# Products of keys and values on the two column halves of TensorE: linear attention and a gated feed-forward in one kernel

## The chip, the cores and the metric

The kernel runs on one core of a Trainium2 chip. The core has a matrix engine (TensorE, PE in the profile; its weight loads are listed as PEld), a vector engine (VectorE, DVE), an activation engine (ScalarE, ACT), GpSimd (POOL) and SyncE (SP). TensorE reads its operands from SBUF and writes to PSUM, from which VectorE and ScalarE copy results back. Each engine works through its own list of instructions in order and waits on the others by semaphores; transfers from and to the chip's memory are issued on queues of SP and POOL. The metric is the device time of one execution in microseconds (us), lower is better.

## The reference, cut to what matters

```python
# q, k, v: (8 batches, 8 heads, 576 positions, 64)
phi = lambda x: np.where(x > 0, x, np.exp(x) - 1.0) + 1.0
q_p, k_p = phi(q), phi(k)
kv  = np.einsum('bhsd,bhse->bhde', k_p, v)      # per head: 64x64
z   = np.sum(k_p, axis=2)                       # per head: 64
num = np.einsum('bhsd,bhde->bhse', q_p, kv)
den = np.einsum('bhsd,bhd->bhs', q_p, z)[..., None] + 1e-06
x   = (num / den).transpose(0, 2, 1, 3).reshape(8 * 576, 512)
a, b = x @ w1, x @ w2                           # 512 -> 1024
out = (a * b @ w3) @ w_out                      # 1024 -> 1024 -> 512
```

Since nothing stands between the last two products, the kernel forms w3 @ w_out once and applies it as one matrix of 1024x512.

## The kernel before, in words

**Tiling.** Each batch has 576 positions: 512 of them make four tiles of 128 (index j, 0 to 3), and the 64 that remain are put together two batches at a time (names that end in r; kr and vrz hold keys and values of the remainder, and vrz is zero outside its own batch's rows). Heads go in pairs: hp is 0 to 3, with u = 0, 1 for the two heads of a pair. phi is max(x, 0) + 1 on VectorE (step t), exp on ScalarE (step x), and the minimum of the two on VectorE (step m, one for each pair, 128x512). Values are copied to bf16 into one buffer, vt, which has a column of ones behind each head's 64 columns, so that a product with keys gives kv and z together: 65 columns for a head (E1), 130 for a pair (PW).

**The product kv.** Step kv takes one batch and one pair. Its weights are the keys of both heads of the pair (128 positions x 128 columns), its moving operand the values of both heads (130 columns), and it makes five matmuls that accumulate in PSUM: four for j (L238) and one for the remainder (L241). The result is 128x130, of which the diagonal blocks, head 0's keys with head 0's values and head 1's with head 1's, are wanted; the two others are computed and not read. Steps kc (two or four pairs) and kh (one pair) copy the wanted blocks to the tile kvb, one copy for each half r of the rows, on ScalarE (a) or VectorE (v). kvb is zero outside its diagonal blocks.

**What follows.** Step na multiplies the queries of a pair with its kvb (four matmuls of 130 columns, L291), nd divides by the denominator on VectorE (L297 to L299) into xn, and xp with xc, or a transposing DMA (xd), turns the result into xt. Step f is a feed-forward step: for one block of 128 columns it makes four matmuls of 512 columns with w1 (a_ps) and four with w2 (b_ps) (L400). ac copies a_ps to SBUF on ScalarE (L414), ab multiplies it with b_ps on VectorE (L419). Step o makes eight matmuls of 512 columns (L425), one for each ab block in the order 0 to 7; oc copies its result out and st stores it. PSUM is used as four banks in turn for f, o and the transposes (mm_ps) and two double banks in turn for kv and na (at_ps).

**The order of the work.** It is written out by hand. The string ORDER is read from left to right; each word, such as `kv:2,1` (batch 2, pair 1) or `ab:1,5` (batch 1, block 5), appends the instructions of its step to the lists of the engines it uses. The tool that builds the kernel adds semaphore waits where one step needs another's data or buffer, and leaves the order as it is. So a step placed later stands later in its engine's list. Attention of batch b + 1 and later stands among the feed-forward steps of batch b and before. The kv products of batches 2 to 7 stand, one or two at a time, among f, o and xp steps. `v:3,0,4,v` copies heads 0 to 3 of batch 3's values into vt on VectorE; as vt is a single buffer, it follows the products of batch 2 that read these heads. GATES adds a few waits between loads and is not concerned.

Of the kernel before, what the change touches and what calls it, by code (L numbers as in the profile page):

```python
# [18 lines left out]
def kernel(  # L19
# [376 lines left out]
    def f_part(c, f, cs):  # L396
        for n, w in (("a", w1_sb), ("b", w2_sb)):
            o = got(ps, (n, c, f), mm_ps, [P, NCH], F32, "mm", n + "_ps")
            for kc in cs:
                nc.tensor.matmul(o, w[:, kc, f * P:(f + 1) * P], xt_of(c)[:, :, kc, :],  # L400
                                 start=(kc == 0), stop=(kc == KC - 1))
# [80 lines left out]
    st:0,3,g x:k,2,0,4 kv:2,2 ab:1,7 f:1,0 m:k,2,0,1 m:k,2,0,0 ac:1,0,a t:q,2,0,4 x:q,2,0,4 kv:2,0 f:1,4
    ab:1,0 x:q,2,4,4 ld:q,3,0,8,s t:q,2,4,4 m:q,2,0,0 ac:1,4,a m:q,2,0,1 f:1,6 m:q,2,4,2 m:q,2,4,3
    ab:1,4 ac:1,6,a qd:2 f:1,2 ab:1,6 ac:1,2,a kv:2,1 ab:1,2 f:1,1 v:3,0,4,v ac:1,1,a f:1,3 x:q,3,4,4
    t:q,3,0,4 lp:v,2,s ab:1,1 ac:1,3,a tr:k,2,2 xr:k,2,2 t:q,3,4,4 f:1,5 ld:k,3,0,8,s x:q,3,0,4 ab:1,3
# [5 lines left out]
    kc:3,0,2,0,v st:1,2,g x:q,4,4,4 kc:3,0,2,1,v f:2,0 vr:5,v t:q,4,4,4 ac:2,0,a f:2,1 ab:2,0 ac:2,1,a
    m:q,4,4,2 m:q,4,0,0 na:3,0 m:q,4,0,1 na:3,2 f:2,6 ab:2,1 nd:3,2 ac:2,6,a nd:3,0 f:2,4 v:4,4,4,a
    v:4,0,4,v ab:2,6 ac:2,4,a na:3,3 m:q,4,4,3 ld:k,4,0,8,s na:3,1 ab:2,4 f:2,7 lp:k,3,s nd:3,3 ac:2,7,a
    nd:3,1 qd:4 f:2,3 ab:2,7 ac:2,3,a f:2,2 ab:2,3 ac:2,2,a t:k,4,0,4 x:k,4,4,4 f:2,5 t:k,4,4,4
    x:k,4,0,4 ab:2,2 ld:k,5,0,8,s xd:3 m:k,4,4,2 ac:2,5,a m:k,4,4,3 kv:4,2 m:k,4,0,0 kv:4,3 ab:2,5 o:2,2
    m:k,4,0,1 xr:k,3,2 tr:k,3,2 kv:4,1 mr:k,3,2 oc:2,2,a kv:4,0 o:2,3 kc:4,0,2,0,a st:2,2,g kc:4,0,2,1,a
    na:4,0 oc:2,3,a na:4,3 o:2,1 nd:4,0 x:k,5,0,4 st:2,3,g nd:4,3 ld:q,5,0,8,s x:k,5,4,4 t:k,5,4,4
    na:4,1 na:4,2 oc:2,1,a o:2,0 nd:4,1 st:2,1,g m:k,5,4,2 nd:4,2 ld:v,5,0,8,s oc:2,0,a t:k,5,0,4 xd:4
    st:2,0,g m:k,5,0,1 m:k,5,4,3 m:k,5,0,0 f:3,7 ac:3,7,a f:3,2 ab:3,7 ac:3,2,a x:q,5,4,4 t:q,5,0,4
    f:3,4 ab:3,2 x:q,5,0,4 t:q,5,4,4 f:3,3 m:q,5,4,2 ac:3,4,a m:q,5,0,1 ab:3,4 ac:3,3,a lp:v,3,s  # L500
    m:q,5,4,3 v:5,4,4,a m:q,5,0,0 f:3,0 ab:3,3 v:5,0,4,a qd:5 ac:3,0,a kv:5,3 kv:5,0 ab:3,0 kv:5,1
    kv:5,2 f:3,6 kc:5,0,2,0,a kc:5,0,2,1,v ac:3,6,a ld:v,6,0,8,s f:4,6 ab:3,6 ac:4,6,a f:4,7 ab:4,6
    vr:6,a vr:7,v ac:4,7,a f:4,3 ab:4,7 ac:4,3,a na:5,2 na:5,0 ab:4,3 f:4,0 nd:5,2 v:6,0,4,a v:6,4,4,v
    ac:4,0,a lp:q,0,s na:5,3 nd:5,0 f:4,4 ab:4,0 ld:q,6,0,8,s ac:4,4,a nd:5,3 ld:k,6,0,8,s f:4,1 ab:4,4
    ac:4,1,a f:4,2 ld:v,7,0,8,s ab:4,1 ac:4,2,a f:4,5 ab:4,2 x:q,6,4,4 t:q,6,4,4 t:q,6,0,4 x:q,6,0,4
    f:3,1 m:q,6,4,2 m:q,6,4,3 ac:4,5,a m:q,6,0,0 m:q,6,0,1 ac:3,1,a ab:4,5 o:4,0 qd:6 x:k,6,4,4 ab:3,1
    t:k,6,0,4 x:k,6,0,4 o:4,3 t:k,6,4,4 oc:4,0,a tr:q,0,2 xr:q,0,2 m:k,6,4,2 st:4,0,g m:k,6,4,3
    ld:k,7,0,8,s m:k,6,0,1 kv:6,2 oc:4,3,v o:4,2 mr:q,0,2 st:4,3,g m:k,6,0,0 kv:6,0 oc:4,2,v kv:6,1
    qdr:0 kv:6,3 v:7,0,4,a o:4,1 st:4,2,g kc:6,0,2,1,v v:7,4,4,v kc:6,0,2,0,v na:5,1 oc:4,1,v f:3,5
    nd:5,1 st:4,1,g ac:3,5,a xd:5 na:6,0 na:6,3 ab:3,5 o:3,1 nd:6,3 nd:6,0 o:3,3 oc:3,1,v x:k,7,0,4  # L510
    t:k,7,4,4 st:3,1,g ld:q,7,0,8,s x:k,7,4,4 t:k,7,0,4 o:3,0 m:k,7,0,1 oc:3,3,a m:k,7,0,0 m:k,7,4,2
    st:3,3,g m:k,7,4,3 kv:7,0 oc:3,0,a kv:7,2 kv:7,3 st:3,0,g kv:7,1 o:3,2 kc:7,0,2,1,v kc:7,0,2,0,v
    na:6,2 oc:3,2,v na:6,1 f:5,7 nd:6,1 st:3,2,g nd:6,2 ac:5,7,a f:5,6 xd:6 ab:5,7 ac:5,6,a nar:0 nar:1
    ab:5,6 f:5,3 x:q,7,4,4 t:q,7,4,4 lp:q,1,s x:q,7,0,4 ndr:1 f:5,2 m:q,7,4,3 ac:5,3,a m:q,7,4,2 ab:5,3
    ac:5,2,a t:q,7,0,4 f:5,4 m:q,7,0,0 ab:5,2 ac:5,4,a m:q,7,0,1 ndr:0 qd:7 f:6,1 ab:5,4 ac:6,1,a f:6,7
    xdr:0 ab:6,1 ac:6,7,a lp:q,2,s f:6,4 ab:6,7 lp:q,3,s ac:6,4,a f:6,2 ab:6,4 ac:6,2,a na:7,3 na:7,2
    ab:6,2 f:6,6 nd:7,2 xr:q,1,2 tr:q,1,2 ac:6,6,a mr:q,1,2 f:6,5 nd:7,3 qdr:1 ab:6,6 ac:6,5,a na:7,0
    f:5,1 ab:6,5 nd:7,0 ac:5,1,a f:6,0 ab:5,1 ac:6,0,a f:5,0 ab:6,0 xr:q,2,2 tr:q,2,2 ac:5,0,a mr:q,2,2
    na:7,1 qdr:2 f:5,5 ab:5,0 xr:q,3,2 tr:q,3,2 nd:7,1 ac:5,5,a nar:2 mr:q,3,2 xd:7 nar:3 ab:5,5 o:5,1
    ndr:2 ndr:3 o:5,0 qdr:3 oc:5,1,a st:5,1,g xdr:1 o:5,2 oc:5,0,a st:5,0,g o:5,3 oc:5,2,a st:5,2,g  # L520
    f:7,0 oc:5,3,a st:5,3,g ac:7,0,a nar:4 f:7,6 ab:7,0 ndr:4 ac:7,6,a nar:5 f:7,3 ab:7,6 ndr:5 ac:7,3,a
    xdr:2 nar:7 f:7,1 ab:7,3 ac:7,1,a ndr:7 f:7,4 ab:7,1 ac:7,4,a f:7,7 ab:7,4 ac:7,7,a nar:6 f:7,5
    ab:7,7 ndr:6 ac:7,5,a xdr:3 f:7,2 ab:7,5 ac:7,2,a f:6,3 ab:7,2 ac:6,3,a o:7,1 ab:6,3 o:7,2 oc:7,1,a
    st:7,1,s o:6,1 oc:7,2,a st:7,2,s f:8,5 oc:6,1,a st:6,1,s ac:8,5,a f:8,0 ab:8,5 ac:8,0,a f:8,3 ab:8,0
    ac:8,3,a f:8,6 ab:8,3 ac:8,6,a f:8,7 ab:8,6 ac:8,7,a f:8,1 ab:8,7 ac:8,1,a ab:8,1 o:6,0 o:6,3
# [44 lines left out]
```

## Time and profile before

| | |
|---|---|
| median of 5 runs | 252.67 us (252.09 to 252.85) |
| the profiled execution | 252.16 us, span from first to last instruction 250.3 us |
| TensorE busy | 238.4 us (95%), granted clock 1.00 |
| VectorE, ScalarE busy | 164.2 us (66%), 122.4 us (49%) |
| kv matmuls, L238 and L241 | 128 and 32, records of 220 ns each |
| their weight loads | 160, records of 97 and 98 ns |
| f matmuls of batches, L400 a_ps and b_ps | 256 and 256 recorded, 379 ns each |
| copies to kvb of four pairs' halves, L248 | 64x260: 0.42 us on VectorE, 0.37 us on ScalarE |
| where the kv products of batches 2 to 7 stand | between 66.5 and 158.7 us |

The profile's span is counted from the first instruction. Busy time is the union of an engine's records. Matmuls are pipelined: a record is longer than the step from one matmul to the next, so the pace of TensorE is read from the starts in its timeline. A line of the timeline gives the start, the length from the first start to the last end of a run of equal instructions, the engine, the source line, the operation with what it writes and reads, and the number of instructions; what stands in brackets is idle time before it and the engine that ended it. In the groups of the page, the numbers after the first bar are busy time and mean ns of one, those after the second the idle time before and its main cause.

### The profile page before, as it was taken

The numbers are of one execution on the slowest core, as the hardware profiler recorded it, in microseconds if no ns is written. First come the engines' busy times: TensorE is split into PE (matmuls) and PEld (weight loads), VectorE is DVE, ScalarE is ACT, GpSimd is POOL, SyncE is SP. The second block draws the span as 40 slices with busy tenths as digits, with TensorE's granted clock in tenths as the row PEclk, the third lists the DMA queues.
The fourth block names the chain that finished last, engine by engine and source line by source line (L and its number), as shares of the span: only waits on it lengthen the run. The fifth ranks groups of instructions, "written<-read, shape, count | busy, mean of one in ns | idle before, by whom it ended". The sixth has DMA issues, their size and how long they took to land.

```text
span 250.3 us, 4088 instructions
## 1 busy us (share of the span) xinstructions
PE 238.4 (95%) x1500; PEld 126.9 (51%) x1516; DVE 164.2 (66%) x364; ACT 122.4 (49%) x190; POOL 35.9 (14%) x59
## 2 busy tenths in 40 slices
PE   8897889979999999999999999999999999999994
PEld 8653854445544555454544454544544444444442
DVE  7517764877878999959648889686775365042320
...
PEclk9999999999999999999999999999999999999999
...
GB/s 118 203 263 348 215 198 296 305 255 328 296 267 248 329 299 208 237 229 364 217 273 346 119 268 227 288 161 125 100 10 131 181 22 21 87 42 27 57 144 152
DMA packets 69620, 50.08 MB, mean 200 GB/s; under 512 B 41312, under 2 KB 64096, under 8 KB 69600
## 3 DMA queue, kind: packets, MB, share of 16 engines
...
q8 instruction: 12, 0.20, 0.3%
...
q14 instruction: 8, 0.07, 0.1%
...
## 4 chain that ended last, share of the span: by engine, by line
PE 71%; DMA 19%; DVE 5%; ACT 1%; issue 1%; POOL 1%; POOLq 0%; ACTq 0%
PE b_ps L400 22%; PE a_ps L400 22%; PE o_ps L425 20%; DMA v<-in_v_dram 8%; DMA q<-in_q_dram 4%; DMA w_sb<-in_moe_w_dram 4%; DMA wo<-in_moe_w_out_dram 3%; PE kvp L238 2%; DVE xn L299 2%; PE nd L291 2%; POOL w3b L159 1%; PE ndr L316 1%; PE o_ps L452 1%; DVE r L298 1%; PE kvp L241 1%
## 5 line engine op out<-in xcount | busy, mean ns | idle before, releaser
L400 PEld LDWEIGHTS <-w_sb 128*128 128x128 bf16 x576 | 55.6, 98 | 63.9 <-issue 0.8
L419 DVE TENSOR_TENSOR ab<-a_sb,b_ps 128x512 bf16<-128x512 f32 x72 | 49.0, 685 | 44.7 <-PE b_ps L400 41.5
L414 ACT COPY a_sb<-a_ps 128x512 f32<-128x512 f32 x72 | 42.0, 584 | 59.6 <-PE a_ps L400 54.9
L400 PE MATMUL a_ps<-xt,w_sb 128*128 128x512 bf16 x256 | 66.0, 379 | 0.5 <-ACT xt L338 0.5
L400 PE MATMUL b_ps<-xt,w_sb 128*128 128x512 bf16 x256 | 66.0, 379 | 0.0
L425 PE MATMUL o_ps<-wf_sb,ab 128*128 128x512 bf16 x267 | 62.7, 379 | 0.7 <-DVE ab L419 0.2
L425 PEld LDWEIGHTS <-ab 128*128 128x128 bf16 x280 | 26.7, 98 | 29.2 <-DVE ab L419 0.3
L443 POOL DMA_DIRECT2D out_dram<-o_sb x24 | 14.1, 586 | 149.8 <-ACT o_sb L431 131.0
L431 ACT COPY o_sb<-o_ps 128x512 f32<-128x512 f32 x24 | 14.0, 584 | 34.4 <-PE o_ps L425 31.9
L299 DVE TENSOR_TENSOR xn<-nd,r 128x512 bf16<-128x512 f32 x32 | 22.1, 692 | 1.1
L166 ACT ACTIVATE e<-q 128x1024 bf16<-128x1024 f32 x16 | 16.5, 1056 | 1.4 <-DMA q<-in_q_dram 1.4
L166 ACT ACTIVATE e<-k 128x1024 bf16<-128x1024 f32 x16 | 16.4, 1058 | 0.8 <-DMA k<-in_k_dram 0.8
L217 ACT CAST vt<-v 128x1024 bf16<-128x1024 f32 (+1 forms) x11 | 10.2, 934 | 5.7 <-PE kvp L238 3.1
L238 PE MATMUL kvp<-vt,k 128*128 128x130 bf16 x128 | 11.2, 220 | 1.8 <-ACT vt L217 1.2
L431 DVE COPY o_sb<-o_ps 128x512 f32<-128x512 f32 x11 | 7.6, 688 | 8.1 <-PE o_ps L425 8.0
L180 DVE TENSOR_TENSOR k<-t,e 128x512 bf16<-128x512 bf16 x32 | 12.3, 421 | 0.6 <-ACT e L166 0.3
L180 DVE TENSOR_TENSOR q<-t,e 128x512 bf16<-128x512 bf16 x32 | 11.9, 421 | 0.2
L238 PEld LDWEIGHTS <-k 128*128 128x128 bf16 x128 | 9.0, 97 | 5.6 <-issue 2.4
L291 PE MATMUL nd<-kvb,qt 128*128 128x130 bf16 x128 | 10.9, 220 | 1.0 <-DVE kvb L248 0.4
L172 DVE TENSOR_SCALAR t<-q 128x1024 bf16<-128x1024 f32 x16 | 11.0, 690 | 0.8 <-DMA q<-in_q_dram 0.7
L172 DVE TENSOR_SCALAR t<-k 128x1024 bf16<-128x1024 f32 x16 | 10.5, 688 | 1.3 <-DMA k<-in_k_dram 1.3
L113 PE MATMUL warm<-zero 128*128 128x128 bf16 x116 | 10.0, 255 | 1.2 <-DVE zero L96 1.2
...
## 6 DMA issues: line engine op xcount, KB each, us to landing
...
```

The source lines that it names most:

```text
L166: return nc.scalar.activation(out=e[:, 0:nh * W], in_=raw[n, b][:, h0 * W:(h0 + nh) * W], func=AF.Exp)
L172: nc.vector.tensor_scalar(out=d[:, 0:nh * W], in0=raw[n, b][:, h0 * W:(h0 + nh) * W], scalar1=0.0, scalar2=1.0, op0=ALU.max, op1=ALU.add)
L180: nc.vector.tensor_tensor(out=d[:, hp].rearrange("p j u d -> p u j d"), in0=ts[n, b, h0][:, s].rearrange("p (u j d) -> p u j d", u=2, j=NJ ...
L238: nc.tensor.matmul(dst, kj[:, hp, j].rearrange("p u d -> p (u d)"), vt[:, j, 2 * hp:2 * hp + 2, :].rearrange("p h e -> p (h e)"), start=(j ...
L291: nc.tensor.matmul(o[:, j // 2, (j % 2) * 256:(j % 2) * 256 + PW], sb["qt", b][:, hp, j * P:(j + 1) * P], kvb[b][:, hp].rearrange("p u e - ...
L299: nc.vector.tensor_tensor(out=dst, in0=o[:, :, :, 0:D], in1=r.unsqueeze(3).to_broadcast(list(r.shape) + [D]), op=ALU.mult)
L400: nc.tensor.matmul(o, w[:, kc, f * P:(f + 1) * P], xt_of(c)[:, :, kc, :], start=(kc == 0), stop=(kc == KC - 1))
L414: return copy_of[eng](out=d, in_=ps["a", c, f])
L419: nc.vector.tensor_mul(out=d[:, f, :], in0=sb["a", c, f], in1=ps["b", c, f])
L425: nc.tensor.matmul(d, sb["ab", c][:, f, m * P:(m + 1) * P], wf_sb[:, f, :], start=(f == 0), stop=(f == FC - 1))
L431: return copy_of[eng](out=d, in_=ps["o", c, m])
L443: queue_of[queue].dma_start(out=dst, in_=sb["o", c, m][r])
```

## The change

Two steps are added. kk does for batches 2 to 7 what kv did: for each pair and each of the five parts it makes two matmuls, one for each head u, with that head's 64 columns of keys as weights and that head's 65 columns of values as the moving operand. Head 0 writes the PSUM rows 0 to 63, head 1 the rows 64 to 127, so that each uses one half of the array's columns. Both write the same 65 PSUM columns, and the four pairs of a batch lie side by side in one bank (260 columns). The blocks off the diagonal are not computed. kg copies a half of the rows, 64x260, to kvb. Batches 0 and 1 keep kv, kc and kh.

In ORDER the four kk of a batch stand together. The steps that were between its kv products keep their order among themselves, except `v:3,0,4,v`, which moves behind them.

```diff
+    @step
+    def kk(b, hp):
+        o = got(ps, ("kk", b), at_ps, [P, 2, 512], F32, "at", "kvp")[:, 0]
+        kj, kr, vt = ph["k", b], ph["kr", b // 2, 2], vts[b % len(vts)]
+        for j in range(NJ + 1):
+            for u in range(2):
+                h = 2 * hp + u
+                nc.tensor.matmul(o[u * D:(u + 1) * D, hp * E1:(hp + 1) * E1],
+                                 kj[:, hp, j, u] if j < NJ else kr[:, h * D:(h + 1) * D],
+                                 vt[:, j, h] if j < NJ else vrz[:, b % 2, h],
+                                 start=(j == 0), stop=(j == NJ))
+
+    @step
+    def kg(b, r, eng):
+        rows = slice(r * D, (r + 1) * D)
+        copy_of[eng](out=kvb[b][rows, :, r, :], in_=ps["kk", b][rows, 0, 0:KC * E1].rearrange(
+            "p (c e) -> p c e", e=E1))
```

The order, with the words that move, set out by batch (unmoved words between them are left out):

```diff
 batch 2
-f:1,7 ... kv:2,2 ab:1,7 f:1,0 ... kv:2,0 f:1,4 ... kv:2,1 ab:1,2 f:1,1 v:3,0,4,v ac:1,1,a ... mr:k,2,2 ac:1,5,a kv:2,3 ld:q,4,0,8,s ab:1,5 o:1,1 kc:2,0,2,0,a kc:2,0,2,1,a
+f:1,7 ... ab:1,7 f:1,0 ... f:1,4 ... ab:1,2 f:1,1 ac:1,1,a ... mr:k,2,2 ac:1,5,a kk:2,0 kk:2,1 kk:2,2 kk:2,3 v:3,0,4,v ld:q,4,0,8,s ab:1,5 o:1,1 kg:2,0,a kg:2,1,a
 batch 3
-nd:2,1 kv:3,3 xp:2,3 x:q,4,0,4 m:k,3,0,1 kv:3,0 xp:2,1 t:q,4,0,4 kv:3,1 xc:2,3,a kv:3,2 oc:1,2,v ... kc:3,0,2,0,v ... kc:3,0,2,1,v f:2,0
+nd:2,1 xp:2,3 x:q,4,0,4 m:k,3,0,1 xp:2,1 t:q,4,0,4 xc:2,3,a kk:3,0 kk:3,1 kk:3,2 kk:3,3 oc:1,2,v ... kg:3,0,v ... kg:3,1,v f:2,0
 batch 4
-m:k,4,4,3 kv:4,2 m:k,4,0,0 kv:4,3 ab:2,5 o:2,2 m:k,4,0,1 xr:k,3,2 tr:k,3,2 kv:4,1 mr:k,3,2 oc:2,2,a kv:4,0 o:2,3 kc:4,0,2,0,a st:2,2,g kc:4,0,2,1,a
+m:k,4,4,3 m:k,4,0,0 ab:2,5 o:2,2 m:k,4,0,1 xr:k,3,2 tr:k,3,2 mr:k,3,2 oc:2,2,a kk:4,0 kk:4,1 kk:4,2 kk:4,3 o:2,3 kg:4,0,a st:2,2,g kg:4,1,a
 batch 5
-kv:5,3 kv:5,0 ab:3,0 kv:5,1 kv:5,2 f:3,6 kc:5,0,2,0,a kc:5,0,2,1,v
+ab:3,0 kk:5,0 kk:5,1 kk:5,2 kk:5,3 f:3,6 kg:5,0,a kg:5,1,v
 batch 6
-o:4,3 ... kv:6,2 oc:4,3,v o:4,2 ... m:k,6,0,0 kv:6,0 oc:4,2,v kv:6,1 qdr:0 kv:6,3 v:7,0,4,a o:4,1 st:4,2,g kc:6,0,2,1,v v:7,4,4,v kc:6,0,2,0,v
+o:4,3 ... oc:4,3,v o:4,2 ... m:k,6,0,0 oc:4,2,v qdr:0 kk:6,0 kk:6,1 kk:6,2 kk:6,3 v:7,0,4,a o:4,1 st:4,2,g kg:6,1,v v:7,4,4,v kg:6,0,v
 batch 7
-m:k,7,0,1 oc:3,3,a m:k,7,0,0 m:k,7,4,2 st:3,3,g m:k,7,4,3 kv:7,0 oc:3,0,a kv:7,2 kv:7,3 st:3,0,g kv:7,1 o:3,2 kc:7,0,2,1,v kc:7,0,2,0,v
+m:k,7,0,1 oc:3,3,a m:k,7,0,0 m:k,7,4,2 st:3,3,g m:k,7,4,3 oc:3,0,a st:3,0,g kk:7,0 kk:7,1 kk:7,2 kk:7,3 o:3,2 kg:7,1,v kg:7,0,v
```

More of the change, by code (lines that the diff above doesn't have):

```diff
@@ L481 @@
     xc:1,3,a mr:k,1,2 x:k,2,4,4 t:k,2,0,4 f:1,7 lp:k,2,s t:k,2,4,4 oc:0,3,a m:k,2,4,2 ac:1,7,a m:k,2,4,3
[L482 to L485, printed above, removed]
@@ L486 @@
-    mr:k,2,2 ac:1,5,a kv:2,3 ld:q,4,0,8,s ab:1,5 o:1,1 kc:2,0,2,0,a kc:2,0,2,1,a v:3,4,4,v m:q,3,0,0
+    st:0,3,g x:k,2,0,4 ab:1,7 f:1,0 m:k,2,0,1 m:k,2,0,0 ac:1,0,a t:q,2,0,4 x:q,2,0,4 f:1,4 ab:1,0
+    x:q,2,4,4 ld:q,3,0,8,s t:q,2,4,4 m:q,2,0,0 ac:1,4,a m:q,2,0,1 f:1,6 m:q,2,4,2 m:q,2,4,3 ab:1,4
+    ac:1,6,a qd:2 f:1,2 ab:1,6 ac:1,2,a ab:1,2 f:1,1 ac:1,1,a f:1,3 x:q,3,4,4 t:q,3,0,4 lp:v,2,s ab:1,1
+    ac:1,3,a tr:k,2,2 xr:k,2,2 t:q,3,4,4 f:1,5 ld:k,3,0,8,s x:q,3,0,4 ab:1,3 mr:k,2,2 ac:1,5,a kk:2,0
@@ L487 @@
+    kk:2,1 kk:2,2 kk:2,3 v:3,0,4,v ld:q,4,0,8,s ab:1,5 o:1,1 kg:2,0,a kg:2,1,a v:3,4,4,v m:q,3,0,0
     m:q,3,4,3 na:2,2 m:q,3,0,1 oc:1,1,a na:2,0 o:1,3 m:q,3,4,2 nd:2,0 st:1,1,g qd:3 nd:2,2 xp:2,0
     oc:1,3,a o:1,0 t:k,3,4,4 vr:4,a st:1,3,g t:k,3,0,4 x:k,3,4,4 xp:2,2 x:k,3,0,4 na:2,3 m:k,3,4,2
-    na:2,1 m:k,3,4,3 o:1,2 nd:2,3 oc:1,0,a xc:2,2,a st:1,0,g m:k,3,0,0 xc:2,0,a nd:2,1 kv:3,3 xp:2,3
-    x:q,4,0,4 m:k,3,0,1 kv:3,0 xp:2,1 t:q,4,0,4 kv:3,1 xc:2,3,a kv:3,2 oc:1,2,v xc:2,1,a ld:v,4,0,8,s
@@ L491 @@
[L491 to L525, printed above, removed]
@@ L526 @@
-    oc:6,0,a st:6,0,s f:8,2 oc:6,3,a st:6,3,s ac:8,2,a f:8,4 ab:8,2 ac:8,4,a o:6,2 ab:8,4 o:8,3 oc:6,2,v
-    st:6,2,s o:8,1 oc:8,3,a st:8,3,s o:8,0 oc:8,1,a st:8,1,s o:8,2 oc:8,0,v st:8,0,s o:7,0 oc:8,2,v
-    st:8,2,s oc:7,0,a st:7,0,s ol:7,3
+    na:2,1 m:k,3,4,3 o:1,2 nd:2,3 oc:1,0,a xc:2,2,a st:1,0,g m:k,3,0,0 xc:2,0,a nd:2,1 xp:2,3 x:q,4,0,4
+    m:k,3,0,1 xp:2,1 t:q,4,0,4 xc:2,3,a kk:3,0 kk:3,1 kk:3,2 kk:3,3 oc:1,2,v xc:2,1,a ld:v,4,0,8,s
+    kg:3,0,v st:1,2,g x:q,4,4,4 kg:3,1,v f:2,0 vr:5,v t:q,4,4,4 ac:2,0,a f:2,1 ab:2,0 ac:2,1,a m:q,4,4,2
@@ new lines @@
+    m:q,4,0,0 na:3,0 m:q,4,0,1 na:3,2 f:2,6 ab:2,1 nd:3,2 ac:2,6,a nd:3,0 f:2,4 v:4,4,4,a v:4,0,4,v
+    ab:2,6 ac:2,4,a na:3,3 m:q,4,4,3 ld:k,4,0,8,s na:3,1 ab:2,4 f:2,7 lp:k,3,s nd:3,3 ac:2,7,a nd:3,1
+    qd:4 f:2,3 ab:2,7 ac:2,3,a f:2,2 ab:2,3 ac:2,2,a t:k,4,0,4 x:k,4,4,4 f:2,5 t:k,4,4,4 x:k,4,0,4
+    ab:2,2 ld:k,5,0,8,s xd:3 m:k,4,4,2 ac:2,5,a m:k,4,4,3 m:k,4,0,0 ab:2,5 o:2,2 m:k,4,0,1 xr:k,3,2
+    tr:k,3,2 mr:k,3,2 oc:2,2,a kk:4,0 kk:4,1 kk:4,2 kk:4,3 o:2,3 kg:4,0,a st:2,2,g kg:4,1,a na:4,0
@@ new lines @@
+    oc:2,3,a na:4,3 o:2,1 nd:4,0 x:k,5,0,4 st:2,3,g nd:4,3 ld:q,5,0,8,s x:k,5,4,4 t:k,5,4,4 na:4,1
+    na:4,2 oc:2,1,a o:2,0 nd:4,1 st:2,1,g m:k,5,4,2 nd:4,2 ld:v,5,0,8,s oc:2,0,a t:k,5,0,4 xd:4 st:2,0,g
+    m:k,5,0,1 m:k,5,4,3 m:k,5,0,0 f:3,7 ac:3,7,a f:3,2 ab:3,7 ac:3,2,a x:q,5,4,4 t:q,5,0,4 f:3,4 ab:3,2
+    x:q,5,0,4 t:q,5,4,4 f:3,3 m:q,5,4,2 ac:3,4,a m:q,5,0,1 ab:3,4 ac:3,3,a lp:v,3,s m:q,5,4,3 v:5,4,4,a
+    m:q,5,0,0 f:3,0 ab:3,3 v:5,0,4,a qd:5 ac:3,0,a ab:3,0 kk:5,0 kk:5,1 kk:5,2 kk:5,3 f:3,6 kg:5,0,a
@@ new lines @@
+    kg:5,1,v ac:3,6,a ld:v,6,0,8,s f:4,6 ab:3,6 ac:4,6,a f:4,7 ab:4,6 vr:6,a vr:7,v ac:4,7,a f:4,3
+    ab:4,7 ac:4,3,a na:5,2 na:5,0 ab:4,3 f:4,0 nd:5,2 v:6,0,4,a v:6,4,4,v ac:4,0,a lp:q,0,s na:5,3
+    nd:5,0 f:4,4 ab:4,0 ld:q,6,0,8,s ac:4,4,a nd:5,3 ld:k,6,0,8,s f:4,1 ab:4,4 ac:4,1,a f:4,2
+    ld:v,7,0,8,s ab:4,1 ac:4,2,a f:4,5 ab:4,2 x:q,6,4,4 t:q,6,4,4 t:q,6,0,4 x:q,6,0,4 f:3,1 m:q,6,4,2
+    m:q,6,4,3 ac:4,5,a m:q,6,0,0 m:q,6,0,1 ac:3,1,a ab:4,5 o:4,0 qd:6 x:k,6,4,4 ab:3,1 t:k,6,0,4
+    x:k,6,0,4 o:4,3 t:k,6,4,4 oc:4,0,a tr:q,0,2 xr:q,0,2 m:k,6,4,2 st:4,0,g m:k,6,4,3 ld:k,7,0,8,s
@@ new lines @@
+    m:k,6,0,1 oc:4,3,v o:4,2 mr:q,0,2 st:4,3,g m:k,6,0,0 oc:4,2,v qdr:0 kk:6,0 kk:6,1 kk:6,2 kk:6,3
+    v:7,0,4,a o:4,1 st:4,2,g kg:6,1,v v:7,4,4,v kg:6,0,v na:5,1 oc:4,1,v f:3,5 nd:5,1 st:4,1,g ac:3,5,a
+    xd:5 na:6,0 na:6,3 ab:3,5 o:3,1 nd:6,3 nd:6,0 o:3,3 oc:3,1,v x:k,7,0,4 t:k,7,4,4 st:3,1,g
+    ld:q,7,0,8,s x:k,7,4,4 t:k,7,0,4 o:3,0 m:k,7,0,1 oc:3,3,a m:k,7,0,0 m:k,7,4,2 st:3,3,g m:k,7,4,3
+    oc:3,0,a st:3,0,g kk:7,0 kk:7,1 kk:7,2 kk:7,3 o:3,2 kg:7,1,v kg:7,0,v na:6,2 oc:3,2,v na:6,1 f:5,7
@@ new lines @@
+    nd:6,1 st:3,2,g nd:6,2 ac:5,7,a f:5,6 xd:6 ab:5,7 ac:5,6,a nar:0 nar:1 ab:5,6 f:5,3 x:q,7,4,4
+    t:q,7,4,4 lp:q,1,s x:q,7,0,4 ndr:1 f:5,2 m:q,7,4,3 ac:5,3,a m:q,7,4,2 ab:5,3 ac:5,2,a t:q,7,0,4
+    f:5,4 m:q,7,0,0 ab:5,2 ac:5,4,a m:q,7,0,1 ndr:0 qd:7 f:6,1 ab:5,4 ac:6,1,a f:6,7 xdr:0 ab:6,1
+    ac:6,7,a lp:q,2,s f:6,4 ab:6,7 lp:q,3,s ac:6,4,a f:6,2 ab:6,4 ac:6,2,a na:7,3 na:7,2 ab:6,2 f:6,6
+    nd:7,2 xr:q,1,2 tr:q,1,2 ac:6,6,a mr:q,1,2 f:6,5 nd:7,3 qdr:1 ab:6,6 ac:6,5,a na:7,0 f:5,1 ab:6,5
@@ new lines @@
+    nd:7,0 ac:5,1,a f:6,0 ab:5,1 ac:6,0,a f:5,0 ab:6,0 xr:q,2,2 tr:q,2,2 ac:5,0,a mr:q,2,2 na:7,1 qdr:2
+    f:5,5 ab:5,0 xr:q,3,2 tr:q,3,2 nd:7,1 ac:5,5,a nar:2 mr:q,3,2 xd:7 nar:3 ab:5,5 o:5,1 ndr:2 ndr:3
+    o:5,0 qdr:3 oc:5,1,a st:5,1,g xdr:1 o:5,2 oc:5,0,a st:5,0,g o:5,3 oc:5,2,a st:5,2,g f:7,0 oc:5,3,a
+    st:5,3,g ac:7,0,a nar:4 f:7,6 ab:7,0 ndr:4 ac:7,6,a nar:5 f:7,3 ab:7,6 ndr:5 ac:7,3,a xdr:2 nar:7
+    f:7,1 ab:7,3 ac:7,1,a ndr:7 f:7,4 ab:7,1 ac:7,4,a f:7,7 ab:7,4 ac:7,7,a nar:6 f:7,5 ab:7,7 ndr:6
@@ new lines @@
+    ac:7,5,a xdr:3 f:7,2 ab:7,5 ac:7,2,a f:6,3 ab:7,2 ac:6,3,a o:7,1 ab:6,3 o:7,2 oc:7,1,a st:7,1,s
+    o:6,1 oc:7,2,a st:7,2,s f:8,5 oc:6,1,a st:6,1,s ac:8,5,a f:8,0 ab:8,5 ac:8,0,a f:8,3 ab:8,0 ac:8,3,a
+    f:8,6 ab:8,3 ac:8,6,a f:8,7 ab:8,6 ac:8,7,a f:8,1 ab:8,7 ac:8,1,a ab:8,1 o:6,0 o:6,3 oc:6,0,a
+    st:6,0,s f:8,2 oc:6,3,a st:6,3,s ac:8,2,a f:8,4 ab:8,2 ac:8,4,a o:6,2 ab:8,4 o:8,3 oc:6,2,v st:6,2,s
+    o:8,1 oc:8,3,a st:8,3,s o:8,0 oc:8,1,a st:8,1,s o:8,2 oc:8,0,v st:8,0,s o:7,0 oc:8,2,v st:8,2,s
@@ L529 @@
+    oc:7,0,a st:7,0,s ol:7,3
     """
```

## The prediction

> **What bounds the kernel now.** I read four views in this order: the 40 slices of the page, the chain that ended last, the list of who made TensorE wait, and the timeline of TensorE around each place where a kv product stands. From the page of the kernel before, the span and busy times, the slices of TensorE with its granted clock, and the chain by engine (other rows left out):
>
> ```profile
> span 250.3 us, 4088 instructions
> PE 238.4 (95%) x1500; PEld 126.9 (51%) x1516; DVE 164.2 (66%) x364; ACT 122.4 (49%) x190; POOL 35.9 (14%) x59
> ...
> PE   8897889979999999999999999999999999999994
> ...
> PEclk9999999999999999999999999999999999999999
> ...
> PE 71%; DMA 19%; DVE 5%; ACT 1%; issue 1%; POOL 1%; POOLq 0%; ACTq 0%
> ```
>
> TensorE is full from slice 11 on, the granted clock is full throughout, and the chain is TensorE but for the start, which waits on DMA. The changed work lies between 61 and 162 us. There TensorE is busy 100.19 of 101.00 us, and the waits put down to others come to 0.4 us. So whatever the change adds to TensorE's time there moves the end by as much; after 162 us the list of waits is empty, so nothing later can take a delay up.
>
> How fast a matmul follows the one before is read from starts, not from record lengths, which include the pipeline. Timeline of TensorE, batch 5 (start, length, what):
>
> ```profile
> 122.62 0.39 PE L238 MATMUL kvp<-vt,k 128*128 128x130 bf16 x4
> 122.85 0.22 PE L241 MATMUL kvp<-vrz,kr 128*128 128x130 bf16 x1
> 122.90 0.39 PE L238 MATMUL kvp<-vt,k 128*128 128x130 bf16 x4
> ...
> 123.70 0.22 PE L241 MATMUL kvp<-vrz,kr 128*128 128x130 bf16 x1
> 123.75 0.59 PE L400 MATMUL a_ps<-xt,w_sb 128*128 128x512 bf16 x2
> ```
>
> Twenty matmuls of 130 columns take 123.75 - 122.62 = 1.13 us, 56.5 ns each; all six batches together are 120 x 56.5 = 6.8 us. The same reading of eight 512-column matmuls (113.99 to 115.71) gives 216 ns. A straight line through both is 2.2 ns + 0.4175 ns per column. The weight loads, one for each matmul, are hidden at this pace: the page's group of them (busy time and mean ns of one, then idle time before) shows 97 ns for one, longer than the step from matmul to matmul.
>
> ```profile
> L238 PEld LDWEIGHTS <-k 128*128 128x128 bf16 x128 | 9.0, 97 | 5.6 <-issue 2.4
> ```
>
> **The change, part by part.**
>
> *The pairs.* Each of the 120 matmuls of 128x130 becomes two of 64x65, each with its own 64-column weight load: 240 matmuls and 240 loads for 120 and 120. No row shows a matmul on half of the columns, so I bound a pair. From below: if the halves overlap fully, a pair costs one 65-column matmul, 2.2 + 65 x 0.4175 = 29.4 ns. In between: if they follow one another at the line's pace, 58.8 ns. From above: if a load with its matmul costs half a pair whatever its width, what the 128x130 one costs, 113 ns; if each load stands in the open, 97 + 29 = 126 per half, 253 per pair. Issue looks like no obstacle: in the timeline of weight loads below, after a wait, the first load starts at 157.45, the hundredth in which its matmul starts too, and four loads of 97 ns are through in 0.23 us.
>
> ```profile
> 157.45 0.23 PEld L238 LDWEIGHTS <-k 128*128 128x128 bf16 x4 [0.45 <-DVE k L180]
> 157.63 0.10 PEld L241 LDWEIGHTS <-kr 128*128 128x128 bf16 x1
> ```
>
> I take 58.8, because it is the only value that rests on rows that agree among themselves (130 and 512 columns, loads hidden): 120 x (58.8 - 56.5) = **+0.28 us**. The ends are 120 x (29.4 - 56.5) = -3.25, +6.8 and +23.6 us.
>
> The record above of a 128-column load (97 ns, hidden at a pace of 56.5) is where a rule speaks against this change: the Trainium skill, "TensorEngine Tiling (Array Packing)", section Restrictions, says that column tiling switches the fast weight load off. "TensorE: Matmul & The Clock Gate", section "LDWEIGHTS (loading the stationary operand)", prices a plain load at columns / 1.2 ns, which makes 53 ns for 64 columns, an estimate; two in a row would make a pair 107 ns and this term +6.0 us instead of +0.28. No row before the change can tell which holds.
>
> *Entering and leaving the split array.* Six stretches, so 12 changes between the whole array and two halves. Today a change of operand, width or PSUM bank costs nothing (L400 follows L241 at 56 ns, 123.70 to 123.75). If a change of partition must let the array run empty, it costs the tail of a matmul beyond its pace: 220 - 56.5 = 163 ns for 130 columns, 379 - 216 = 163 ns for 512. Ends: 0 and 12 x 0.163 = 1.96 us. I take the upper, since a 64-column load cannot be laid under a matmul that fills all 128 columns in the way that the rows show for equal shapes: **+1.96 us**. The Trainium skill, "TensorEngine Tiling (Array Packing)", section Key Properties, states such a drain at a mode switch; without it this term would be 0, and the trace of before shows neither.
>
> *The moved order.* ScalarE, SP and GpSimd keep their instructions in the same order, DMA issues included; VectorE has one moved copy (below). On TensorE the four products of a batch now stand together, at the place where its last one or a middle one stood. Products that filled a wait leave it open. Batch by batch, at the old pace:
>
> ```profile
> 87.99 0.39 PE L238 MATMUL kvp<-vt,k 128*128 128x130 bf16 x4
> 88.21 0.22 PE L241 MATMUL kvp<-vrz,kr 128*128 128x130 bf16 x1
> 88.27 0.39 PE L333 MATMUL xtp<-ident,xn 128*128 128x128 bf16 x4
> ...
> 89.15 0.40 PE L333 MATMUL xtp<-ident,xn 128*128 128x128 bf16 x4 [0.21 <-DVE xn L299]
> 89.49 0.40 PE L238 MATMUL kvp<-vt,k 128*128 128x130 bf16 x4
> ```
>
> - Batch 3: two products (0.57 us) stood ahead of the transposes at 89.15, which wait for VectorE's xn (88.41 + 0.69). That end does not move. After: 89.15 + 0.23 of transposes + 1.13 of kv = 90.51, where the next matmul (L400) began at 90.06: **+0.45**. (Product 1 no longer waits for its k, done at 89.43, as it did in 89.49 against 89.38.)
> - Batch 4: two products (0.57) stood between the feed-forward step and o:2,2, from 104.78 to 105.35. Its sixth matmul needs the ab that VectorE writes from 105.39 to 106.08, being busy up to there. After, that matmul is due at 104.78 + 5 x 0.216 = 105.86 and can go at 106.08 + 0.06 (a VectorE end to TensorE's start, 157.39 to 157.45): **+0.28**.
> - Batch 7: products wait one by one for k tiles that VectorE gives in the order 1, 0, 2, 3 (1.25 us from 157.45 to 158.70). In the order 0, 1, 2, 3 none waits: 1.13, **-0.12**.
> - Batches 5 and 6 have their products in other orders whose inputs are ready (vt by 122.6, k by 146.8 where it is wanted at 146.9): 0. Batch 2 had three of its four among the feed-forward steps, which do not wait for evacuation (VectorE's ab for step 7 ends at 67.5, its bank is wanted at 69.1): 0.
> - The moved copy: v:3,0,4 (heads 0 to 3 of the single vt buffer, 0.69 us) now waits for kk:2,0 and 2,1 and has ab:1,5 behind it, which o:1,1 needs at its sixth matmul. Read to 79.32, copied by 80.07, ab by 80.75, plus 0.06, against 80.81 due: just covered by the other half of the kv stretch and five matmuls of o; 0. If that cover shrinks, as with fast pairs, some 0.2 us show.
> - The kvb copies kg take the same 64x260 elements as kc (0.42 VectorE, 0.37 ScalarE) under the same o or f steps: 0.
>
> Sum: 0.28 + 1.96 + 0.45 + 0.28 - 0.12 = **+2.85 us**. The profiled execution took 252.16 us (span 250.3 and 1.9 around it), so 255.0 beside it; it lay 0.5 below the median of the runs, so against that 252.67 + 2.85 = **255.5 us**.
>
> **Rivals.**
>
> *The halves run at the same time (ends on the other side: faster).* For it: nothing in the two halves shares a column, and starts after a wait follow closely. Against it: every matmul in the trace follows its predecessor by its full column count, so overlap is not seen anywhere. Price: -3.25 + 0.61 of order + 0.2 for the copy = -2.44 with free changes of partition, -0.48 with full ones: 250.2 to 252.2. The point from which it decides: with free changes a pair under 51 ns (0.61 / 120 = 5 below 56.5), with full ones under 35 ns.
>
> *The number of loads becomes the bound.* A load and matmul of half the width cost as much as a whole one: 113 ns a pair, 6.8 + 0.61 + 1.96 = +9.4, 262.0 us; with free changes 260.1. For it: twice the instructions on an engine without slack, and loads that need a matmul long enough to hide under, here 29 instead of 57 ns. Against it: the close starts at 157.45, shown above.
>
> *The loads cannot hide at all on a half.* 253 ns a pair: 23.6 + 2.6 = +26.2, 278.9 us. For it: only that half-array loads are not shown; against it: hidden loads everywhere else.
>
> **How the numbers follow.** Pairs near the serial pace (45 to 75 ns), changes from free to full: 0.45. Its own range is 253.5 (no drain) to 257.5 (75 ns: 2.2 + 0.61 + 1.96 = 4.8). Overlapping halves 0.24, load-bound 0.25, open loads 0.06. A change under 0.2% (0.5 us) is about what a measurement of this kernel can't tell from none. Faster is the first rival but for its slow end: 0.20. Within 0.2%: that end and the no-drain end of the forecast: 0.07. Slower: 0.73. The range that holds 8 in 10 goes from 250.6, which cuts only the best of the overlapping case, to 262.2, which takes the load-bound case in and leaves out the open loads.
>
> **What would show it.** In the timeline of TensorE, the start of kk's first matmul to the start of its successor, over 20, is the pair: 59 ns for my forecast, 29 to 35 for overlap, 110 for loads. The start of the first 64x65 matmul against the one before, beyond that one's pace, and likewise on leaving, is the change of partition: 0.16 us each. The waits of o on ab near 106 and of the transposes near 89 show the order's part. Wrong would make it: pairs below 50 ns, a change that costs more than a tail, or weight loads of 64 columns that take as long as those of 128.

## The result, and the profile after

The changed kernel is faster: 251.76 us, the median of 54 runs (250.73 to 253.74), beside 252.45 for 94 runs of the kernel before; the ratio is 0.9968, with a 95% interval of 0.9958 to 0.9978. The forecast was 255.5 us, slower, and its range began at 250.6: the time lies inside the range and on the other side of no change.

The page of the changed kernel, its span and busy times and its chain by engine:

```profile
span 249.4 us, 4327 instructions
PE 236.9 (95%) x1620; PEld 123.6 (50%) x1636; DVE 163.9 (66%) x364; ACT 122.7 (49%) x190; POOL 36.2 (15%) x59
...
PE 70%; DMA 19%; DVE 5%; ACT 2%; issue 2%; POOL 1%; ACTq 0%; POOLq 0%
```

TensorE still ends the chain, with 120 matmuls more and 1.5 us of busy time less. The profiled execution took 251.14 us. The timeline of TensorE at batch 5, where the kernel before took 1.13 us from 122.62 to 123.75:

```profile
121.59 1.03 PE L420 MATMUL b_ps<-xt,w_sb 128*128 128x512 bf16 x4
122.60 0.32 PE L254 MATMUL kvp<-vt,k 128*64 128x65 bf16 x8
122.72 0.22 PE L254 MATMUL kvp<-vrz,kr 128*64 128x65 bf16 x2
122.75 0.32 PE L254 MATMUL kvp<-vt,k 128*64 128x65 bf16 x8
...
123.20 0.23 PE L254 MATMUL kvp<-vrz,kr 128*64 128x65 bf16 x2
123.36 1.04 PE L420 MATMUL a_ps<-xt,w_sb 128*128 128x512 bf16 x4
```

Ten matmuls of a product start within 0.15 or 0.16 us (122.60, 122.75), so a pair takes 32 ns, and the next matmul on the whole array starts 0.76 us after the first pair. Two gaps are new: b_ps is through at 121.59 + 0.86 = 122.45 and the first pair starts at 122.60, and after the last product (10 matmuls from 123.07 to 123.23) the next matmul waits until 123.36. Of the first gap, 0.05 us is a wait for the values; the rest comes back at every stretch. The two views of the same instructions by line show that the weight loads have a length of their own:

```profile
L254 PEld LDWEIGHTS <-k x192: 106/112/114, 78.6 to 157.6; 128*64 128x64 bf16 x192
L254 PE MATMUL kvp<-vt,k x192: 190/196/218, 78.6 to 157.6; 128*64 128x65 bf16 x192
```

A load of 64 columns is recorded with 112 ns (median), longer than the 97 of one of 128 columns, and still hidden.

The kernel's start varies by some tenths from one execution to the next (no run here shows why), so the traces are compared over one stretch: from the first matmul of f:1,7 (64.78 us in the trace before) to the first of na:6,2 behind batch 7 (160.43). It takes 95.65 us before and 94.83 after (64.66 to 159.49). What follows takes 86.23 us from there to the start of the last matmul, in all traces of this study. So the trace gained 0.82 us, all of it inside this stretch. By batch, from the starts of the matmuls around each place: batch 2 -0.27, o:1,1 and the transposes behind it +0.18, batch 3 +0.03, batch 4 +0.02, batch 5 -0.22, batch 6 -0.27, batch 7 -0.29.

### The profile page after: what moved, and what is told of

Read it like the earlier page. It is cut to its first block, busy times and chain, and to the rows that moved or that the text cites. A ratio compares the mean times of both kernels' runs of the same rounds, so it can differ in the third digit from the quotient of the medians.

```text
span 249.4 us, 4327 instructions
## 1 busy us (share of the span) xinstructions
PE 236.9 (95%) x1620; PEld 123.6 (50%) x1636; DVE 163.9 (66%) x364; ACT 122.7 (49%) x190; POOL 36.2 (15%) x59
## 4 chain that ended last, share of the span: by engine, by line
PE 70%; DMA 19%; DVE 5%; ACT 2%; issue 2%; POOL 1%; ACTq 0%; POOLq 0%
PE a_ps L420 22%; PE b_ps L420 21%; PE o_ps L445 20%; DMA v<-in_v_dram 8%; DMA q<-in_q_dram 5%; DMA w_sb<-in_moe_w_dram 4%; DMA wo<-in_moe_w_out_dram 3%; DVE xn L319 2%; PE nd L311 2%; PE kvp L254 2%; POOL w3b L159 1%; ACT e L166 1%; PE ndr L336 1%; PE o_ps L472 1%; DVE r L318 1%
## 5 line engine op out<-in xcount | busy, mean ns | idle before, releaser
L180 DVE TENSOR_TENSOR k<-t,e 128x512 bf16<-128x512 bf16 x32 | 12.3, 421 | 0.4 <-ACT e L166 0.2
L311 PEld LDWEIGHTS <-qt 128*128 128x128 bf16 x128 | 8.7, 98 | 4.9 <-DVE xn L319 1.0
L113 PEld LDWEIGHTS <-zero 128*128 128x128 bf16 x116 | 9.0, 118 | 1.4 <-DVE zero L96 1.2
```

Source lines behind the costliest of these rows:

```text
L113: nc.tensor.matmul(t[:, 0:P], zero[:, 0:P], zero[:, 0:P], start=True, stop=True)
L180: nc.vector.tensor_tensor(out=d[:, hp].rearrange("p j u d -> p u j d"), in0=ts[n, b, h0][:, s].rearrange("p (u j d) -> p u j d", u=2, j=NJ ...
L311: nc.tensor.matmul(o[:, j // 2, (j % 2) * 256:(j % 2) * 256 + PW], sb["qt", b][:, hp, j * P:(j + 1) * P], kvb[b][:, hp].rearrange("p u e - ...
```

## The experiments

All of them are changes of these two kernels. The stretch of the table is the one just defined; where stretches are counted ("six stretches"), runs of products on the halves are meant.

| kernel | median, runs | ratio to before (95%) | stretch, us |
|---|---|---|---|
| before | 252.45 (94) | | 95.65 |
| after | 251.76 (54) | 0.9968 (0.9958 to 0.9978) | 94.83 |
| order alone | 253.14 (12) | 1.0013 (0.9986 to 1.0039) | 96.42 |
| halves in place | 252.88 (12) | 1.0002 (0.9973 to 1.0030) | 95.98 |
| half by half | 252.20 (12) | 0.9979 (0.9943 to 1.0014) | 97.97 |
| one half | 255.26 (1) | | 98.37 |
| left, then right | 254.21 (1) | | 97.97 |
| covers mended | 253.01 (12) | 1.0004 (0.9969 to 1.0038) | 97.42 |
| covers mended, 2 | 251.99 (12) | 0.9993 (0.9966 to 1.0020) | 95.28 |
| covers mended, 3 | 250.88 (12) | 0.9947 (0.9918 to 0.9977) | 94.19 |
| after, again | 251.55 (12) | 0.9987 (0.9961 to 1.0013) | 94.80 |
| after, a third time | 252.15 (12) | 0.9979 (0.9956 to 1.0002) | 95.38 |

### The order alone

```diff
-    kk:2,0 kk:2,1 kk:2,2 kk:2,3 ... kg:2,0,a kg:2,1,a      (and so on for batches 3 to 7)
+    kv:2,0 kv:2,1 kv:2,2 kv:2,3 ... kc:2,0,2,0,a kc:2,0,2,1,a
```

> The order of the changed kernel, with the whole-array products of before (128x130, 56.5 ns each) and their copies in place of the halves. Theory (the halves overlap at 32 ns a pair and save 2.94 us; the moved order and the changes of partition give part of it back): the order alone costs 0.45 (transposes near 89 us), 0.28 (o:2,2), some 0.15 (the vt copy moved on VectorE) and gains 0.12 at batch 7: +0.7 to +0.8 us, ratio to before 1.003. Rival (the time fell because the products stand together, not because of the halves): 0.997, as the changed kernel.

Measured: the stretch is 0.77 us longer than before (96.42). TensorE around batch 3 in this run:

```profile
88.96 0.40 PE L353 MATMUL xtp<-ident,xn 128*128 128x128 bf16 x4 [0.77 <-DVE xn L319]
89.19 0.39 PE L238 MATMUL kvp<-vt,k 128*128 128x130 bf16 x4
...
90.33 1.03 PE L420 MATMUL a_ps<-xt,w_sb 128*128 128x512 bf16 x4
```

The transposes now wait 0.77 us with nothing in front of them, and the next step starts 1.37 us behind them, where it was 0.91 before (89.15 to 90.06): +0.46. Batch 4 added 0.28, batch 7 took 0.11 off, and 0.14 was a wait for the values of batch 5. The moved copy cost nothing, where some 0.15 was expected: that the total came out as expected is luck in this part, since the wait at batch 5 took its place. That wait comes from the order. In the kernel before, ScalarE copies the values of batch 5 heads 4 to 7 first, then heads 0 to 3:

```profile
120.71 2.00 ACT L217 CAST vt<-v 128x1024 bf16<-128x1024 f32 x2
```

The second copy ends at 122.71, and the products start at 122.62 with pair 3, which needs only the first copy. In the new order they start with pair 0, which needs the second.

The rival, that standing together is what made the kernel faster, falls: the interval of the ratio leaves out 0.997, and in the trace the new order by itself costs.

### The halves where the products stood

```diff
     (the order of before, for batches 2 to 7)
-    f:1,7 ... kv:2,2 ab:1,7 f:1,0 ... kv:2,0 ... kc:2,0,2,0,a kc:2,0,2,1,a
+    f:1,7 ... kk:2,2 ab:1,7 f:1,0 ... kk:2,0 ... kg:2,0,a kg:2,1,a
```

> The order of before, with pairs of half-array matmuls where the whole-array products of batches 2 to 7 stood: 13 stretches on halves instead of 6. Theory (each stretch costs about 0.21 us: 0.094 on entering, 0.02 in its first pair, 0.10 on leaving): 120 x (32 - 56.5) = -2.94, + 13 x 0.21 = 2.7: -0.2 us, ratio 0.999, so no better than the changed kernel though no cover is lost. Rival (a change of partition costs nothing; the gaps seen are the start of a kv product as such): -2.9 us, ratio 0.988.

Measured: no gain. Two single products on halves, in the timeline of TensorE:

```profile
65.46 1.03 PE L420 MATMUL b_ps<-xt,w_sb 128*128 128x512 bf16 x4
66.42 0.32 PE L254 MATMUL kvp<-vt,k 128*64 128x65 bf16 x8
66.57 0.20 PE L254 MATMUL kvp<-vrz,kr 128*64 128x65 bf16 x2
66.70 1.04 PE L420 MATMUL a_ps<-xt,w_sb 128*128 128x512 bf16 x4
...
68.53 0.32 PE L254 MATMUL kvp<-vt,k 128*64 128x65 bf16 x8
68.67 0.20 PE L254 MATMUL kvp<-vrz,kr 128*64 128x65 bf16 x2
68.81 1.04 PE L420 MATMUL a_ps<-xt,w_sb 128*128 128x512 bf16 x4
```

From one a_ps to the next it is 2.10 and 2.11 us (64.60, 66.70, 68.81), where it was 2.01 with the whole-array product between (64.78, 66.79, 68.80). So one product on halves costs 0.09 to 0.10 us more than on the whole array, although its ten matmuls take 0.16 us and not 0.28. The starts say where it goes: the first pair comes 309 ns after a 512-column matmul instead of 216 (+0.093), the second pair 52 ns after the first instead of 32 (+0.020), the matmul on the whole array 129 ns after the last of the halves instead of about 30 (+0.10), and the one behind it 226 ns later instead of 216 (+0.010). That is 0.22 us for each stretch on the halves, the same in all traces where nothing else is waited for, and a product saves 5 x (56.5 - 32) = 0.12: a stretch pays from two products on. The changed kernel has six stretches of four. Of the 0.33 us by which the trace from 64 to 160 us exceeds before, 0.46 is a wait for the values of batch 5; without it the reading is -0.13, against -0.2 expected. The rival, that a change of partition is free (0.988), falls: the interval begins at 0.9973.

### One half of the array

```diff
-                nc.tensor.matmul(o[u * D:(u + 1) * D, hp * E1:(hp + 1) * E1],
+                nc.tensor.matmul(o[0:D, u * 512 + hp * E1:u * 512 + (hp + 1) * E1],
...
-        copy_of[eng](out=kvb[b][rows, :, r, :], in_=ps["kk", b][rows, 0, 0:KC * E1].rearrange(
+        copy_of[eng](out=kvb[b][rows, :, r, :], in_=ps["kk", b][0:D, r, 0:KC * E1].rearrange(
```

> The changed kernel with both heads of a pair on the left half of the array: head 1's products go to the same 64 PSUM rows in a second bank and are copied from there; the count of matmuls, loads and copies is the same. Theory (each half works through its own list, one 65-column matmul after the other at 29.4 ns or, if the plain 64-column load sets the pace, up to 53; the gain is that two halves run at once): 40 matmuls from first to last 1.15 us, up to 2.1, instead of 0.63; with the six stretches the trace is 3.1 us longer or more from 61 to 162 us. Rival (any 64x65 matmul takes 16 ns of the array): 0.63 us, as in the changed kernel.

Measured: TensorE at batch 5 in this run:

```profile
125.04 0.41 PE L254 MATMUL kvp<-vt,k 128*64 128x65 bf16 x8
...
125.35 0.41 PE L254 MATMUL kvp<-vt,k 128*64 128x65 bf16 x8
...
125.67 0.42 PE L254 MATMUL kvp<-vt,k 128*64 128x65 bf16 x8
...
126.40 0.82 PE L420 MATMUL a_ps<-xt,w_sb 128*128 128x512 bf16 x3
```

Ten matmuls take 0.31 to 0.32 us, twice as long as with both halves; the forty take 1.265 us from first to last start, 0.63 in the changed kernel. The stretch is 3.5 us longer than after. So one half takes a 65-column matmul every 32 ns, its load included, and the gain is that the two halves do so at the same time. The rival (16 ns anywhere) falls. Whether the columns of the array or the 64 PSUM rows that they write set these 32 ns, the run does not separate. The costs of entering and leaving are the same (309, 52 and 130 ns), so they belong to matmuls of 64 columns and not to the use of both halves.

### Half by half, and left then right

```diff
-        for j in range(NJ + 1):
-            for u in range(2):
+        for u in range(2):
+            for j in range(NJ + 1):
```

> The changed kernel with the two loops of a product exchanged: the five matmuls of the left half, then the five of the right, so that neighbours share a half but for one in five. Theory (a pair takes 32 ns because its members stand on different halves and run at once): neighbours on one half follow at 29 to 57 ns, a pair takes 55 to 107 ns: the changed kernel + 2.8 to 9 us, ratio to before 1.008 to 1.033. Rival (a 64x65 matmul takes 16 ns of the array wherever its neighbour stands): as the changed kernel, 0.997.

The theory was wrong here: from first to last start the forty matmuls take 0.69 us, 34 ns a pair, hardly more than in alternation. This is what the rival forecast, but the run on one half rules its reason out. Starts in a strict order can't give 0.69 us. Neighbours on one half are at least 29 ns apart, five of them 4 x 29, and eight such groups one behind the other would need 0.93 us. The names show it too, as the remainder's matmul (from kr) is the fifth of each half:

```profile
80.30 0.34 PE L254 MATMUL kvp<-vt,k 128*64 128x65 bf16 x7
80.44 0.20 PE L254 MATMUL kvp<-vrz,kr 128*64 128x65 bf16 x1
```

Seven matmuls start ahead of the first remainder, where four are written ahead of it: three of the right half went before it. So the list of TensorE, described above as worked through in order, is not started strictly in order here. (The stretch of 97.97 us in this trace holds a wait of VectorE of 3.3 us for the queries of batch 3 and one for the values of batch 5, and says nothing of the pairs.) The second run puts all twenty of the left half first:

```diff
+        for u in range(2) if hp == 0 else ():
+            for h in range(u, H, 2):
+                p = h // 2
+                for j in range(NJ + 1):
...
```

> The changed kernel with a batch's twenty left matmuls first and its twenty right ones behind them. Theory (a matmul may start ahead of earlier ones of the other half, as the starts in the run with five and five suggest): the right list starts well before the left one has ended; first to last between 0.65 and 0.95 us. Rival (matmuls start in the written order, and five and five overlapped only at their seams): 1.15 us, with twenty equal steps of 29 ns, then twenty more.

Measured: 1.16 us from first to last start, and the stretch 3.1 us longer than after, so the theory's 0.95 us at most is missed and the rival has the time right for twenty and twenty, though not the strict order. The starts of one batch, as steps in ns from one to the next, worked out from the trace:

```
52 36 29 30 36 29 30 36 29 30 36 29 30 35 29 35  6 23 30  4 29  3  29 30 36 29 30 36 29 30 36 ...
```

Sixteen steps of one half, then three pairs of short and long steps in which both halves run, then one half again. The names show what meets there, from the third remainder of the left half on:

```profile
78.94 0.19 PE L255 MATMUL kvp<-vrz,kr 128*64 128x65 bf16 x1
78.96 0.29 PE L255 MATMUL kvp<-vt,k 128*64 128x65 bf16 x6
79.09 0.20 PE L255 MATMUL kvp<-vrz,kr 128*64 128x65 bf16 x1
79.09 0.23 PE L255 MATMUL kvp<-vt,k 128*64 128x65 bf16 x2
```

Between the left half's last two remainders four matmuls are written and six start; the right half's first product then has two left before its own remainder. So a matmul may start before earlier ones of the other half, but only by a few places: the right half's first starts with the seventeenth of the left, three places ahead of its turn. That is enough for five and five, not for twenty and twenty. A record does not name its half; that the first short step (6 ns) is this first start is argued from its place.

### The lost covers

Three kernels try to give back the waits that the new order opened. The first:

```diff
-    kk:2,3 v:3,0,4,v ... kg:2,1,a v:3,4,4,v ... t:k,3,4,4 vr:4,a ... ac:2,6,a nd:3,0
+    kk:2,3 ... kg:2,1,a v:3,0,4,a v:3,4,4,v ... t:k,3,4,4 ... ac:2,6,a vr:4,a nd:3,0
...
+        fs = (0, 1, 2, 3, 4, 6, 7, 5) if (c, m) == (2, 2) else range(FC)
```

> The changed kernel with three covers given back: the copy v:3,0,4 and the copy vr:4 are on ScalarE where it is idle (the first was on VectorE's full stretch, the second stood ahead of the exponentials of keys 3), and o:2,2 adds its block 5 last. Theory (the lost covers hold 0.2 at 83 us, 0.6 at 88 us and 0.27 at 105 us of TensorE's waits): 0.5 to 0.9 us less than the changed kernel, ratio to before 0.994. Rival (those waits only move to the next full engine, VectorE): as the changed kernel, 0.997.

Measured: 253.01 us, ratio 1.0004; the interval (0.9969 to 1.0038) leaves out the 0.994 that was expected. In its trace the wait of o:2,2 is gone (0.3 us), but VectorE waited 2.8 us for the queries of batch 3, and TensorE 1.5 us at batch 5 for a copy that itself waited 1.4 us for the load of its values. The second leaves vr:4 where it was, keeps the two other moves (not shown again) and mends batch 3 by putting its stretch into the wait:

```diff
-    m:k,3,0,0 xc:2,0,a nd:2,1 xp:2,3 x:q,4,0,4 m:k,3,0,1 xp:2,1 t:q,4,0,4 xc:2,3,a kk:3,0 kk:3,1 kk:3,2 kk:3,3 oc:1,2,v
+    m:k,3,0,0 xc:2,0,a m:k,3,0,1 nd:2,1 xp:2,3 x:q,4,0,4 kk:3,0 kk:3,1 kk:3,2 kk:3,3 xp:2,1 t:q,4,0,4 xc:2,3,a oc:1,2,v
...
+            cs = (0, 2, 3, 1) if (c, f) == (2, 0) else cs
```

> The changed kernel with its lost covers given back in another way: o:2,2 adds its block 5 last; the stretch of batch 3 stands in the wait ahead of the transposes near 89 us, with product 1's keys made before the division that these wait for, and the first step of the next feed-forward part takes its late block of x last; v:3,0,4 is copied on ScalarE behind kg. Nothing else moves. Theory (lost covers): 0.3 + 0.45 + 0.15 less than the changed kernel in the trace from 61 to 162 us, ratio to before 0.994. Rival (VectorE, nearly full there, sets the pace and the waits move on): within 0.2 us of the changed kernel, 0.997.

Measured: ratio 0.9993 (0.9966 to 1.0020), so the 0.994 that was expected is missed. Up to batch 4 the trace is 0.65 us better than after (0.18 at the transposes of batch 2, 0.18 at batch 3 where 0.45 was expected, 0.29 at batch 4), and then loses 1.1 at batch 5. ScalarE, then TensorE in that run:

```profile
121.68 1.99 ACT L217 CAST vt<-v 128x1024 bf16<-128x1024 f32 x2 [1.01 <-DMA v<-in_v_dram]
```
```profile
121.61 1.03 PE L421 MATMUL b_ps<-xt,w_sb 128*128 128x512 bf16 x4
123.72 0.32 PE L254 MATMUL kvp<-vt,k 128*64 128x65 bf16 x8 [1.09 <-ACT vt L217]
```

The load of 1 MB was issued at 109.0 and its data came 12.6 us later; in the windows from 61 to 126 us the DMA engines are busy all the time (share 1.04 to 1.13 in every run). Before the change these copies did not wait for the load, ended at 122.71, and the products started at 122.62: there was no slack left at that place. The third kernel therefore also takes the product of batch 5 two steps later:

```diff
-    v:5,4,4,a m:q,5,0,0 f:3,0 ab:3,3 v:5,0,4,a qd:5 ac:3,0,a ab:3,0 kk:5,0 kk:5,1 kk:5,2 kk:5,3 f:3,6 kg:5,0,a kg:5,1,v ac:3,6,a ld:v,6,0,8,s f:4,6 ab:3,6 ac:4,6,a f:4,7
+    m:q,5,0,0 f:3,0 ab:3,3 qd:5 ac:3,0,a ab:3,0 f:3,6 v:5,4,4,a v:5,0,4,a ac:3,6,a ld:v,6,0,8,s f:4,6 ab:3,6 kk:5,0 kk:5,1 kk:5,2 kk:5,3 ac:4,6,a f:4,7 kg:5,0,a kg:5,1,v
```

> The kernel with mended covers of the run covers_mended2, and the product of batch 5 with its copies two feed-forward steps later (behind f:4,6), the copies of its values one step later. Theory (the mended covers do save some 0.65 us up to 120 us, and the load of the values of batch 5, which lands in the full stretch of the transfer queues, takes it back at the product of batch 5): without that wait the trace from 61 to 162 us is 1.3 us shorter than before and 0.5 shorter than the changed kernel; ratio to before 0.994 to 0.995. Rival (transfers bound this part as a whole, and the next load, of the values of batches 6 and 7 or of q and k, takes the gain instead): as the changed kernel, 0.997 to 0.999.

Measured: ratio 0.9947 (0.9918 to 0.9977), and the stretch is 94.19 us, 1.46 less than before and 0.64 less than after. TensorE at batch 5:

```profile
124.13 1.03 PE L421 MATMUL b_ps<-xt,w_sb 128*128 128x512 bf16 x4
125.09 0.32 PE L254 MATMUL kvp<-vt,k 128*64 128x65 bf16 x8
```

The first pair comes 0.96 us after the first of four 512-column matmuls, the bare 3 x 0.216 + 0.309. Ratio and trace are as the theory said. This is the fastest kernel of the study by its median; its interval still overlaps those of the second mended kernel and of the changed kernel, so that it is faster than these, and that the later product makes the difference, is shown by the traces and not by the times. The changed kernel ran beside the last two:

> The changed kernel itself, beside the others on the same chip, for the comparison with the mended one: ratio to before 0.997. In the trace, the stretch from the first feed-forward step of batch 1 that stands behind 64 us to the product of batch 7 is 0.8 us shorter than before, whatever the start brings.

> The changed kernel once more beside the mended one on the same chip: ratio to before 0.997 to 0.999.

Both intervals hold the expected 0.997, and neither alone excludes no change. In the third run, batch 5 waited too:

```profile
122.85 0.32 PE L254 MATMUL kvp<-vt,k 128*64 128x65 bf16 x8 [0.54 <-ACT vt L217]
```

and its stretch is 95.38 us. So part of the change's gain is taken back in some executions by that load.

## Why the prediction was wrong

- **What bounds the kernel**: right. TensorE sets the pace from 61 us to the end, and the difference of 0.82 us at 160 us stays to the last matmul. What it passed over is that inputs which arrive just in time start to be waited for: the copies of batch 5's values had no slack.
- **The pairs: the step that failed.** It took 58.8 ns a pair, +0.28 us; measured are 32 ns, 120 x (32 - 56.5) = -2.94 us. The value was chosen because two rows, of 130 and 512 columns, agreed on a line. Two points always do, but this line holds for a third row too: transposes of 128 columns follow one another at 56 ns. The rows agreed on what one matmul costs when its neighbours use the same columns of the array; no row had neighbours on different columns, so these rows could not speak on overlap at all. For the same reason "overlap is not seen anywhere" was no argument against the rival. The line itself was good: 29.4 ns worked out for one 65-column matmul, 32 measured on one half.
- **The loads**: neither bound by their number nor by their length. The estimate of 53 ns for a plain 64-column load, from the Trainium skill, "TensorE: Matmul & The Clock Gate", section "LDWEIGHTS (loading the stationary operand)", would have made at least 53 ns between matmuls on one half; the run on one half shows 32. The records did grow from 97 to 112 ns, so a load of half the columns is not half a load, but it stays hidden. The prediction took loads as long as those of 128 columns for a sign of being wrong; they are longer and cost nothing.
- **Entering and leaving**: the mechanism was right, the size too large. 0.093 + 0.020 on entering and 0.10 + 0.010 on leaving make 1.34 us for six stretches, against 1.96 taken. The first load of a stretch is not laid under the matmul before it, which began 0.31 us earlier; the line below has it start within 2 ns of its own matmul at 78.56. A drain, which the Trainium skill, "TensorEngine Tiling (Array Packing)", section Key Properties, states without a price, agrees with this; here it costs 0.22 us a stretch, less than two tails of 0.163 us, which were taken.

```profile
78.56 0.20 PEld L254 LDWEIGHTS <-k 128*64 128x64 bf16 x8 [0.42 <-issue]
```

- **The moved order**: right as worked out, but for batch 5. Alone it was 0.46, 0.28 and -0.11 for batches 3, 4 and 7, where 0.45, 0.28 and -0.12 were forecast. Batch 5 was put at 0 with its values ready "by 122.6"; the copy that pair 0 needs ended at 122.71, and the wait was 0.14 alone and 0.05 with the halves. With the halves batches 3 and 4 became 0.30 and 0.28, batch 7 only -0.02, since fast products wait for the k tiles again (0.16 us ahead of the last), and the moved copy cost 0.18, as the prediction had said of fast pairs.
- **The sum** of what was measured: -2.94 + 1.34 + (0.18 + 0.30 + 0.28 - 0.02 + 0.05 for the values of batch 5) = -0.81 us, beside -0.82 in the trace and -0.7 between the medians. This is the first rival with changes of partition at some two thirds of the full price; the prediction priced it at -0.48 us with full changes and -2.44 with free ones, and gave both together 0.24.
- **The range**: it holds the measured time because it took in most of this rival, not because the forecast's mechanism was near. The forecast's own range was also worked out wrongly at its lower end: 253.5 is 58.8 ns without a drain, while the 45 ns that it names would give 251.9.
